# Attention's product of the last 64 keys on all 128 rows, and a planner that counts changes of array shape

## The chip, the cores and the metric

The kernel runs on one core of one Trainium2 chip. The metric is device time in microseconds of one execution. Times shown are of the whole program: attention and two feed-forward layers in one launch.

## The reference, cut to what matters

```python
# q, k, v: (4, 8, 576, 64), tau: 0.02
scores = scale * np.matmul(q, k.transpose(0, 1, 3, 2))
thresh = np.max(scores, axis=-1, keepdims=True) - tau
scores = np.where(scores >= thresh, scores, -1000000000.0)
attn = softmax(scores)                      # exp, divided by the row's sum
x = np.matmul(attn, v)                      # to (2304, 512)
h = x @ w_in;  x = (h * sigmoid(1.702 * h)) @ w_out      # 512 -> 2048 -> 512
h = x @ w_in2; x = (h * tanh(softplus(h))) @ w_out2      # 512 -> 2048 -> 512
```

All of it is float32. The change lies in attention; the two layers come after it and stay as they are.

## The kernel before, in words

**Tiling of attention.** Two heads are taken together (16 pairs of heads, `b` and `hp`). A pair has five groups of queries: four "full" ones of 128 queries of each head, and a "mixed" one that holds the last 64 queries of both heads, 64 rows each. That makes 80 groups. A group goes through four steps on TensorE and the engines behind it:

- `qk` (line 606): scores = q times k. Contraction over 64 rows, one head on rows 0 to 63 and the other on rows 64 to 127, so two small matmuls run side by side. Output in the PSUM tiles `sc`.
- `softmax_a` (line 635 on): VectorE scales, finds the maximum and cuts (L647, L657), GpSimd adds tau (L651), ScalarE takes the exponential (L654). The result is `p`, 576 keys beside each other, head 0 and then head 1.
- `turn` (line 679): TensorE transposes `p` in chunks of 128 keys into the PSUM banks `tb[0]`, `tb[1]`, `tb[2]` (L702). The keys 512 to 575, 64 of each head, are the "rest": one more transpose (L697), of 128 columns for a full group (both heads' rests together), of `m = 64` columns for a mixed one, which has one array of scores only. ScalarE copies the banks to SBUF (L717), the chunks to `pm`, the rest to `pmt`.
- `product` (line 722): transposed `p` times V (L752). For each of five chunks (`c`), two matmuls, one a head, write rows 0 to 63 and 64 to 127 of `av`. Chunks 0 to 3 contract over 128 rows. The rest (c = 4) contracts over 64: for a full product over rows `64 * i` to `64 * i + 63`, for a mixed one over rows 0 to 63. So the rest uses the array as 64 rows by 64 columns, the other chunks as 128 rows by 64 columns. Every float32 matmul leaves two records in the trace. A full product takes two groups at once (256 queries of one head), after every second full group. `av` lies in the halves of `tb[3]` for full products, and in columns 256 to 319 of `tb[2]` for mixed ones. ScalarE copies `av` out (L761).

So TensorE works in shapes, which the trace shows as rows*columns of a form: `64*128` and `64*64` (scores), `128*128` (transposes, and both layers), `128*64` (products, and the mixed rest's transpose), `64*64` (the rests' products).

**The order of the work.** Nothing is ordered by the hardware: `Order` (lines 53 to 196) is a planner. `add` (line 77) records each step with an engine, an estimated duration, what it reads and writes, and a rank. `run` (line 98) simulates the engines: each time an engine is free it takes, of the steps that are ready, the one of the lowest rank (the oldest one at equal rank). The times so found fix the order in which instructions are issued; a step of several matmuls (`steps`) is spread over its duration, and what other engines do in that time is issued in between. On the chip each engine then works through its own list in that order and waits where data are not ready. Ranks: scores of group g have g - 8 (`SF`), its transposes and copies g, a product g + 1.5 (`VR`), where g is the second of its two groups. The early part of `run` also fills TensorE with spare transposes until the first step of `turn` (`keep_warm`).

**Other work beside attention.** From group 40 on, the weights of the first layer are converted on ScalarE, VectorE and GpSimd (`load_w1`, lines L383 to L405), one f-block every five groups. V arrives by one DMA a pair of heads (`prep`, line 599); the host lays it out as 512 columns of the four chunks and 2 x 64 columns of rests (`tail`, line 980 on). After attention, layer 1 (L521, L566) and layer 2 (L521, L927) run on TensorE.

Of the kernel before, what the change touches and what calls it, by code (L numbers as in the profile page):

```python
# [11 lines left out]
F32 = mybir.dt.float32  # L12
# [9 lines left out]
DMA_RATE = 200e3  # L22
SF = 8
PR = 2
AR = 0.1
VR = 1.5
NORM_P = 1.0
# [15 lines left out]
NKQ = 2  # L43
# [9 lines left out]
class Order:  # L53
# [16 lines left out]
    def __init__(self):  # L70
        self.ops = []
        self.writer = {}
        self.readers = {}
        self.fill = None
        self.port = set()

    def add(self, eng, dur, fn, r=(), w=(), rank=0.0, deps=(), nbytes=None, port=False, steps=1):
        n = len(self.ops)
        if port:
            self.port.add(n)  # L80
        before = set(deps)
        for key in r:
            if key in self.writer:
                before.add(self.writer[key])
        for key in w:
            if key in self.writer:
                before.add(self.writer[key])
            before.update(self.readers.get(key, ()))
        for key in r:
            self.readers.setdefault(key, []).append(n)  # L90
        for key in w:
            self.writer[key] = n
            self.readers[key] = []
        before.discard(n)
        self.ops.append((eng, dur, fn, before, rank, nbytes, steps))
        return n

    def run(self):
# [10 lines left out]
        now = {e: [] for e in engines}  # L109
# [5 lines left out]
        wire = 0.0  # L115
        order = []
        port, done = 0.0, 0
        while done < n_ops:
            best = None
            for e in engines:  # L120
                if now[e]:
                    t = free[e]
                elif future[e]:
                    t = max(free[e], future[e][0][0])
                else:
                    continue
                if best is None or t < best[0]:
                    best = (t, e)
            t, e = best
            while future[e] and future[e][0][0] <= t:  # L130
                i = heapq.heappop(future[e])[1]
                heapq.heappush(now[e], (self.ops[i][4], i))
            aside = []
            i = None
            while now[e]:
                item = heapq.heappop(now[e])
                if item[1] in self.port and port > t + 1e-6:
                    aside.append(item)
                    continue
                i = item[1]  # L140
                break
            for item in aside:
                heapq.heappush(now[e], item)
            if i is None:
                free[e] = port
                continue
            done += 1
            _, dur, _, _, _, nbytes, _ = self.ops[i]
            free[e] = end = t + dur
            if i in self.port:  # L150
                port = end
            self.last = max(self.last, end)
            if nbytes is not None:
                wire = end = max(wire, end + DMA_US) + nbytes / DMA_RATE
            order.append((t, i))
            for a in after[i]:
                lat = self.LAT[e][self.ops[a][0]] if dur or nbytes else 0.0
                ready[a] = max(ready[a], end + lat + SLACK)
                left[a] -= 1
                if not left[a]:  # L160
                    heapq.heappush(future[self.ops[a][0]], (ready[a], a))
        self.order = order = sorted(order)
        if self.fill is not None:
            eng, until, dur, fn = self.fill
            at, gaps = 1.2, []
            for t, i in order:
                if i == until:
                    break
                if self.ops[i][0] == eng:
                    n = int((t - at - FG) / dur) if gaps else FI  # L170
                    if n > 0:
                        gaps.append((at, i, n))
                    at = t + self.ops[i][1]
            order = sorted([(t, i, 0) for t, i in order] + gaps)
        else:
            order = [(t, i, 0) for t, i in order]
        events = []
        for t, i, n in order:
            _, dur, fn, *_, steps = self.ops[i]
            if n:  # L180
                events.append((t, len(events), self.fill[3], n))
            elif steps == 1:
                events.append((t, len(events), fn))
            else:
                for k in range(steps):
                    events.append((t + dur * (k + 1) / steps, len(events), next_of, i, k))
# [16 lines left out]
def attention_then_two_ffn_kernel(  # L203
# [21 lines left out]
    nc = tc.nc  # L225
# [357 lines left out]


    kqs = Ring(apool, "kq", NKQ, [128, 2 * S], F32)
    vrs = Ring(apool, "vr", NKQ, [128, 5 * 128], F32)
    pps = Ring(apool, "p", NP // 2, [128, P1 + S + 1], F32)
    sss = Ring(apool, "ss", NSS, [128, S + 5], F32)
    nms = Ring(apool, "nm", 8, [128, 2], F32)
# [9 lines left out]
    def prep(b, hp, rank):  # L599
        kq2, kkq = kqs.next()  # L600
        vr, kvr = vrs.next()
        dma(lambda: nc.sync.dma_start(out=kq2, in_=kq[b, hp]), 589824, w=[kkq], rank=rank)
        dma(lambda: nc.sync.dma_start(out=vr, in_=v[b, hp]), 327680, w=[kvr], rank=rank)
        head[b, hp] = (kq2, vr, kkq, kvr)

    def qk(tl, rank):
# [5 lines left out]
        def mm():  # L612
# [13 lines left out]
                yield  # L626

        n = 4 if kind == "full" else 2
        add("PE", n * 0.25 + 0.25, mm, [kkq], [("sc", i) for i in range(n)], rank,
            steps=4 if kind == "full" else 5)  # L630
        return [(sc[i][:, :, 0:SH], [("sc", 2 * i), ("sc", 2 * i + 1)]) for i in range(n // 2)]

    def softmax_a(sums, ksum, col, rank, bank, pair, i):
# [45 lines left out]
    def turn(tl, ps, pair, rank):  # L679

        kind, b, hp, t = tl
        full = kind == "full"
        if t == 0:
            xo[b, hp] = xos.next()
        if full:
            if t % 2 == 0:
                turned[b, hp] = [pms.next(), pms.next(), pmt.next()]
            plan = [(0, (0, 1), 128), (1, (2, 3), 128), (2, (4,), 128)]
        else:
            turned[b, hp] = [pms.next(), pmt.next()]  # L690
            plan = [(0, (0, 1, 2, 3), 128), (1, (4,), 64)]

        def tr(bank, cs):
            for n, c in enumerate(cs):
                if c == 4:
                    m = 64 * len(ps)
                    nc.tensor.transpose(tb[bank][0:m, 0:128], pair[:, 516:516 + m], ident)  # L697
                    yield
                    continue
                for i in range(len(ps)):  # L700
                    a, c0 = (P1 + 64 if i else 4) + c * 128, (n * len(ps) + i) * 128
                    nc.tensor.transpose(tb[bank][:, c0:c0 + 128], pair[:, a:a + 128], ident)  # L702
                    yield

        for (bank, cs, rows), (pn, kpn) in zip(plan, turned[b, hp]):
            n = 1 if 4 in cs else len(ps) * len(cs)
            cols = 128 * n
            n = add("PE", n * 0.109 + (0.16 if bank == 0 else 0.0), lambda bank=bank, cs=cs: tr(bank, cs),
                ps, [("tb", bank)], rank, steps=max(n, 2))
            if sch.fill is None and WARM:  # L710
                sch.fill = ("PE", n, 0.107, keep_warm)
            src = tb[bank][0:rows, 0:cols]
            dst = pn[0:rows, 0:cols]
            if full:
                dst = pn[0:rows].rearrange("p (g q) -> p g q", q=256)[:, :, t % 2 * 128:t % 2 * 128 + 128]
                src = src.rearrange("p (g q) -> p g q", q=128)
            add("ACT", t_act(cols), lambda src=src, dst=dst: nc.scalar.copy(dst, src),  # L717
                [("tb", bank)], [kpn + (t % 2,)], rank)
        if not full or t % 2:
            product(tl, rank)  # L720

    def product(tl, rank):
# [17 lines left out]
        def mm(cs):  # L740
            for c in cs:
                for i in range(2):
                    rows, vc = slice(0, 128), c * 128 + 64 * i
                    if c < 4 and full:
                        p, a = pn[c // 2], (c % 2 * 2 + i) * 256
                    elif c < 4:
                        p, a = pn[0], c * 128 + i * 64
                    elif full:
                        rows, p, a, vc = slice(64 * i, 64 * i + 64), pn[2], 0, 512
                    else:  # L750
                        rows, p, a = slice(0, 64), pn[1], 64 * i
                    nc.tensor.matmul(  # L752
                        av[64 * i:64 * i + 64], vr[rows, vc:vc + 64], p[rows, a:a + w],
                        start=(c == 0), stop=(c == 4))
                    yield

        for cs, kp in parts:
            add("PE", len(cs) * (0.482 if full else 0.12) + 0.02, lambda cs=cs: mm(cs),
                kp + [kvr], [kav] + ["product"] * full, rank + VR, steps=2 * len(cs))
        x, kx = xo[b, hp]  # L760
        add("ACT", t_act(w), lambda: nc.scalar.copy(x[:, at:at + w], av), [kav],  # L761
            [kx + (j,) for j in ((t - 1, t) if full else (t,))], rank + VR)
# [252 lines left out]
```

## Time and profile before

| what | value |
|---|---|
| time, median of 3 runs | 1086.83 us (1086.48 to 1087.23) |
| the profiled execution, its own time | 1086.56 us |
| its span in the trace | 1084.8 us |
| TensorE matmul busy in the span | 1073.4 us (99%) |
| VectorE, ScalarE, GpSimd busy | 689.7, 647.8, 161.4 us |
| granted clock of TensorE | 1.0 throughout |
| matmuls of attention end, layer 1 begins | about 289 us; last attention matmul at 298.6 us |

"Busy" of TensorE counts each matmul from its start until its result is out, and matmuls overlap, so 99% doesn't say that the array is full. What a matmul costs a full queue is the distance from its start to the next one's start. In the timeline a row merges matmuls of one form: its first column is the first start, so the difference of the first columns of two neighbouring rows is what the earlier one cost the engine.

### The profile page before, as it was taken

The numbers are of one execution on the slowest core, as the hardware profiler recorded it, in microseconds if no ns is written. First come the engines' busy times: TensorE is split into PE (matmuls) and PEld (weight loads), VectorE is DVE, ScalarE is ACT, GpSimd is POOL, SyncE is SP. The second block draws the span as 40 slices with busy tenths as digits, with TensorE's granted clock in tenths as the row PEclk, the third lists the DMA queues.
The fourth block names the chain that finished last, engine by engine and source line by source line (L and its number), as shares of the span: only waits on it lengthen the run. The fifth ranks groups of instructions, "written<-read, shape, count | busy, mean of one in ns | idle before, by whom it ended". The sixth has DMA issues, their size and how long they took to land.

```text
span 1084.8 us, 16166 instructions
## 1 busy us (share of the span) xinstructions
PE 1073.4 (99%) x6068; PEld 844.8 (78%) x6068; DVE 689.7 (64%) x1378; ACT 647.8 (60%) x1033; POOL 161.4 (15%) x182
## 2 busy tenths in 40 slices
PE   9999999999999999999999999999999999999998
PEld 6666666666688888888888889888888888888887
DVE  7888989899978646545642236665555564555544
ACT  5776778888767344444432245686565656555665
POOL 2221223354425003211310000000000000000000
PEclk9999999999999999999999999999999999999999
DMA  2224243434164265374540025500010010010010
GB/s 90 70 68 125 90 129 123 131 115 130 40 198 141 82 220 178 139 257 143 181 142 20 1 80 178 190 1 22 8 40 0 11 39 1 1 40 1 1 39 20
DMA packets 51390, 94.44 MB, mean 87 GB/s; under 512 B 7280, under 2 KB 28016, under 8 KB 51312
## 3 DMA queue, kind: packets, MB, share of 16 engines
q1 hardware_dynamic: 51312, 93.42, 26.6%
q8 instruction: 47, 0.77, 0.3%
q14 instruction: 31, 0.25, 0.1%
HBM read 70.78 MB, written 22.62 MB: 86 GB/s over the span
## 4 chain that ended last, share of the span: by engine, by line
PE 98%; ACT 1%; DVE 0%; DMA 0%; issue 0%; SPq 0%; ACTq 0%; DVEq 0%
PE h L521 36%; PE tb L566 18%; PE tb L927 18%; PE tb L752 9%; PE sc L625 8%; PE tb L702 7%; PE tb L697 1%; DMA kq<-in_kq 0%; ACT pmt L717 0%; ACT p L654 0%; DVE p L657 0%; DVE ss L647 0%; ACT pm L717 0%; DVE o L939 0%; SPq L783 0%
## 5 line engine op out<-in xcount | busy, mean ns | idle before, releaser
L889 ACT ACTIVATE ms<-ms 128x512 f32<-128x512 f32 (+1 forms) x240 | 131.3, 583 | 129.4 <-DVE ms L874 128.3
L521 PE MATMUL h<-xa,wh 128*128 128x512 f32 (+1 forms) x640 | 181.7, 368 | 0.0
L521 PE MATMUL h<-x,wh 128*128 128x512 f32 (+1 forms) x640 | 181.0, 368 | 0.0
L521 PEld LDWEIGHTS h<-x,wh 128*128 128x128 f32 x640 | 116.5, 188 | 20.4
L521 PEld LDWEIGHTS h<-xa,wh 128*128 128x128 f32 x640 | 116.0, 189 | 20.3 <-issue 0.4
L547 ACT ACTIVATE t<-h 128x512 f32<-128x512 f32 (+1 forms) x80 | 44.4, 555 | 142.9 <-PE h L521 142.7
L657 DVE SCALAR_TENSOR_TENSOR p<-ss,nm,p 128x577 f32<-128x577 f32 x144 | 119.4, 851 | 14.5 <-ACT xo L761 6.1
L647 DVE TENSOR_SCALAR_CACHE_REDUCE ss<-sc,nqsc 128x576 f32<-128x576 f32 x144 | 112.4, 813 | 18.6 <-PE sc L625 17.9
L899 DVE TENSOR_TENSOR ms<-ms,hs 128x512 f32<-128x512 f32 (+1 forms) x80 | 50.1, 635 | 116.4 <-ACT ms L889 116.2
L550 DVE SCALAR_TENSOR_TENSOR h<-t,h 128x512 f32<-128x512 f32 (+1 forms) x80 | 51.2, 640 | 111.4 <-ACT t L547 111.2
L566 PE MATMUL tb<-gl,wh 128*128 128x512 f32 (+1 forms) x320 | 117.8, 368 | 0.0
L521 PE MATMUL h<-xa,wl 128*128 128x512 f32 (+1 forms) x320 | 117.7, 368 | 0.0
L566 PE MATMUL tb<-gh,wh 128*128 128x512 f32 (+1 forms) x320 | 117.7, 368 | 0.0
L521 PE MATMUL h<-x,wl 128*128 128x512 f32 (+1 forms) x320 | 117.7, 368 | 0.0
L566 PE MATMUL tb<-gh,wl 128*128 128x512 f32 (+1 forms) x320 | 117.7, 368 | 0.0
L654 ACT ACTIVATE p<-ss,nm 128x576 f32<-128x576 f32 x144 | 109.8, 785 | 11.2 <-DVE ss L647 11.1
L395 POOL TENSOR_TENSOR sv<-sv,sr 128x1024 uint32<-128x1024 uint32 x32 | 84.0, 2628 | 201.3 <-DVE sv L392 152.1
L927 PE MATMUL tb<-wh,g2h 128*128 128x512 f32 x288 | 112.1, 389 | 0.0
L927 PE MATMUL tb<-wl,g2h 128*128 128x512 f32 x288 | 112.1, 389 | 0.0
L927 PE MATMUL tb<-wh,g2l 128*128 128x512 f32 x288 | 112.0, 389 | 0.0
L651 POOL TENSOR_SCALAR nm<-nm,tau_p 128x1 f32<-128x1 f32 x144 | 76.8, 534 | 190.2 <-DVE ss L647 187.0
L889 ACT ACT_TABLE_LOAD x80 | 102.6, 1283 | 1.4
(59 smaller groups left out, 1685.6 us busy)
## 6 DMA issues: line engine op xcount, KB each, us to landing
sr<-in_w_in SPq DMA_DIRECT2D x32, 512.0 KB
sr<-in_w_out SPq DMA_DIRECT2D x32, 512.0 KB
kq<-in_kq SPq DMA_DIRECT2D x16, 576.0 KB
sv<-x_d SPq DMA_DIRECT2D x16, 512.0 KB
w_d<-sv SPq DMA_DIRECT2D x16, 512.0 KB
sv<-w_d SPq DMA_DIRECT2D x16, 512.0 KB
vr<-in_v SPq DMA_DIRECT2D x16, 320.0 KB
x_d<-xo SPq DMA_DIRECT2D x16, 288.0 KB
```

The lines of the kernel that those rows point to most:

```text
L395: lambda: nc.gpsimd.tensor_tensor(bits, bits, word(0), ALU.add), keys, [kval], rank, port=True)
L521: nc.tensor.matmul(hb[dst][:, 0:n], a[:, c, :], x[:, lo, c, 0:n], start=(i == 0), stop=(i == 3 * KD - 1))
L566: nc.tensor.matmul(accs[e][0][:, 0:n], a[:, es], b()[:, 0:n], start=(f == 0 and i == 0), stop=(f == KF - 1 and i == 2), skip_group_check=True,
L625: nc.tensor.matmul(dst, q, kq2[rows, k0:k0 + n], start=True, stop=True)
L647: lambda: nc.vector.tensor_scalar(n3, s3, nqsc, None, ALU.mult, ALU.min, accum_out=nm[:, 0:1]),
L651: lambda: nc.gpsimd.tensor_scalar(nm[:, 1:2], nm[:, 0:1], tau_p, 0.0, ALU.add, ALU.add),
L654: lambda: nc.scalar.activation(p[:, at:at + S], ns[:, 4:4 + S], AF.Exp, bias=nm[:, 0:1], scale=-1.0),
L657: lambda: nc.vector.scalar_tensor_tensor(p[:, whole], ns[:, 3 + i:4 + S + i], nm[:, 1:2], p[:, whole], ALU.is_le, ALU.mult, accum_out=sums ...
L702: nc.tensor.transpose(tb[bank][:, c0:c0 + 128], pair[:, a:a + 128], ident)
L752: nc.tensor.matmul(av[64 * i:64 * i + 64], vr[rows, vc:vc + 64], p[rows, a:a + w], start=(c == 0), stop=(c == 4))
L889: nc.scalar.activation(m()[:, 0:n], m()[:, 0:n], fn, bias=bias)
L927: nc.tensor.matmul(accs[t][0], x[:, t * 128:(t + 1) * 128], w, start=(f == 0 and i == 0), stop=(f == KF - 1 and i == 2), skip_group_check= ...
```

## The change

The rest's product takes all 128 rows, with zeros in V where a head has nothing; V gets a third tail column block for it. The mixed rest's transpose is 128 columns wide. In the planner, a step on TensorE carries a `mode` (0: transposes and the layers, 1: scores, 2: products). TensorE's choice among ready steps adds `KEEP` = 0.5 to the rank of a step of another mode than the last one, and such a step lasts `TURN` = 0.15 us longer. The estimates of the three kinds of step are new.

```diff
+KEEP = 0.5
+TURN = 0.15
...
+            if e == "PE":
+                item = min(now[e], key=lambda x: (x[0] + KEEP * (self.mode.get(x[1], 0) != held), x[1]))
+                now[e].remove(item)
+                heapq.heapify(now[e])
+                i = item[1]
+            while i is None and now[e]:
...
+            if e == "PE" and self.mode.get(i, 0) != held:
+                held = self.mode.get(i, 0)
+                dur += TURN
+            took[i] = dur
...
-    vrs = Ring(apool, "vr", NKQ, [128, 5 * 128], F32)
+    vrs = Ring(apool, "vr", NKQ, [128, 4 * 128 + 3 * D], F32)
...
-        dma(lambda: nc.sync.dma_start(out=vr, in_=v[b, hp]), 327680, w=[kvr], rank=rank)
+        dma(lambda: nc.sync.dma_start(out=vr, in_=v[b, hp]), 360448, w=[kvr], rank=rank)
...
-        add("PE", n * 0.25 + 0.25, mm, [kkq], [("sc", i) for i in range(n)], rank,
-            steps=4 if kind == "full" else 5)
+        add("PE", 1.02, mm, [kkq], [("sc", i) for i in range(n)], rank,
+            steps=4 if kind == "full" else 5, mode=1)
...
-                    m = 64 * len(ps)
-                    nc.tensor.transpose(tb[bank][0:m, 0:128], pair[:, 516:516 + m], ident)
+                    nc.tensor.transpose(tb[bank][:, 0:128], pair[:, 516:644], ident)
...
-            n = add("PE", n * 0.109 + (0.16 if bank == 0 else 0.0), lambda bank=bank, cs=cs: tr(bank, cs),
+            n = add("PE", n * 0.109, lambda bank=bank, cs=cs: tr(bank, cs),
...
-                    rows, vc = slice(0, 128), c * 128 + 64 * i
+                    vc = c * 128 + 64 * i
...
-                        rows, p, a, vc = slice(64 * i, 64 * i + 64), pn[2], 0, 512
+                        p, a = pn[2], 0
                     else:
-                        rows, p, a = slice(0, 64), pn[1], 64 * i
+                        p, a, vc = pn[1], 64 * i, 512 + 128 * i
                     nc.tensor.matmul(
-                        av[64 * i:64 * i + 64], vr[rows, vc:vc + 64], p[rows, a:a + w],
+                        av[64 * i:64 * i + 64], vr[:, vc:vc + 64], p[:, a:a + w],
...
-            add("PE", len(cs) * (0.482 if full else 0.12) + 0.02, lambda cs=cs: mm(cs),
-                kp + [kvr], [kav] + ["product"] * full, rank + VR, steps=2 * len(cs))
+            add("PE", len(cs) * (0.43 if full else 0.115), lambda cs=cs: mm(cs),
+                kp + [kvr], [kav] + ["product"] * full, rank + VR, steps=2 * len(cs), mode=2)
...
-    tail = _np.zeros((B, H // 2, 128, 2, D), v.dtype)
+    tail = _np.zeros((B, H // 2, 128, 3, D), v.dtype)
     for i in range(2):
-        tail[:, :, 64 * i:64 * i + 64, 0] = vh[:, :, i, 512:]
-    tail[:, :, :64, 1] = vh[:, :, 1, 512:]
+        tail[:, :, 64 * i:64 * i + 64, i] = vh[:, :, i, 512:]
+    tail[:, :, :64, 2] = vh[:, :, 1, 512:]
```

## Rows read from the trace of the kernel before

**Rows 1.** The profile page: the chain that ended last, share of the span by line.

```profile
PE h L521 36%; PE tb L566 18%; PE tb L927 18%; PE tb L752 9%; PE sc L625 8%; PE tb L702 7%; PE tb L697 1%; DMA kq<-in_kq 0%; ACT pmt L717 0%; ACT p L654 0%; DVE p L657 0%; DVE ss L647 0%; ACT pm L717 0%; DVE o L939 0%; SPq L783 0%
```

**Rows 2.** Windows: length; busy PE, PEld, DVE, ACT, POOL; clock, DMA share, GB/s.

```profile
25.00:150.00 125.00, 121.96 (x1006) 77.31 (x1007) 106.27 (x280) 91.62 (x187) 27.82 (x65) 1.00 0.31 91
150.00:288.00 138.00, 135.67 (x1118) 85.07 (x1117) 127.64 (x310) 116.81 (x223) 58.56 (x74) 1.00 0.37 118
```

**Rows 3.** Timeline of TensorE: start, us until the last end, line, form, count.

```profile
199.97 1.08 PE L752 MATMUL tb<-pm,vr 128*64 128x256 f32 x8
200.98 0.65 PE L752 MATMUL tb<-pmt,vr 64*64 64x256 f32 x4
201.56 1.09 PE L702 MATMUL tb<-ident,p 128*128 128x128 f32 x8
202.49 0.27 PE L697 MATMUL tb<-ident,p 128*128 128x128 f32 x1
202.69 1.24 PE L625 MATMUL sc<-kq 64*128 64x288 f32 x8
203.87 0.66 PE L702 MATMUL tb<-ident,p 128*128 128x128 f32 x4
204.36 0.27 PE L697 MATMUL tb<-ident,p 128*64 128x128 f32 x1
204.56 1.95 PE L752 MATMUL tb<-pm,vr 128*64 128x256 f32 x16
206.44 1.24 PE L625 MATMUL sc<-kq 64*128 64x288 f32 x8
207.61 0.65 PE L752 MATMUL tb<-pmt,vr 64*64 64x256 f32 x4
208.19 1.09 PE L702 MATMUL tb<-ident,p 128*128 128x128 f32 x8
...
210.60 0.69 PE L752 MATMUL tb<-pm,vr 128*64 128x64 f32 x16
211.71 0.33 PE L752 MATMUL tb<-pmt,vr 64*64 64x64 f32 x4 [0.42 <-ACT pmt L717]
```

**Rows 4.** The same timeline: first and last full rest right behind its chunks.

```profile
22.03 0.65 PE L752 MATMUL tb<-pmt,vr 64*64 64x256 f32 x4
...
287.15 0.65 PE L752 MATMUL tb<-pmt,vr 64*64 64x256 f32 x4
```

**Rows 5.** Line 752: records, ns of one (min/median/max), first and last start, forms.

```profile
L752 PEld LDWEIGHTS tb<-pm,vr x768: 132/137/138, 17.5 to 298.2; 128*64 128x64 f32 x192
```

**Rows 6.** Timeline of TensorE: a mixed product without a wait.

```profile
156.98 0.69 PE L752 MATMUL tb<-pm,vr 128*64 128x64 f32 x16
157.59 0.33 PE L752 MATMUL tb<-pmt,vr 64*64 64x64 f32 x4
157.86 0.66 PE L702 MATMUL tb<-ident,p 128*128 128x128 f32 x4
```

**Rows 7.** Waits: who waited for whom, us in total, times, longest.

```profile
PE tb L752 <- ACT pmt L717: 4.6, 11, 0.4
```

**Rows 8.** Timeline of TensorE: the first mixed rest whose wait lies at its own start.

```profile
52.01 0.33 PE L752 MATMUL tb<-pmt,vr 64*64 64x64 f32 x4 [0.42 <-ACT pmt L717]
```

**Rows 9.** Timeline of all engines: ScalarE's copy of a rest beside that product.

```profile
211.39 0.27 ACT L717 COPY pmt<-tb 128x128 f32<-128x128 f32 x1 [1.07 <-PE tb L752]
```

**Rows 10.** Timeline of TensorE: transposes that break a product, the first, one, the last.

```profile
18.57 0.66 PE L702 MATMUL tb<-ident,p 128*128 128x128 f32 x4
...
180.47 0.33 PE L697 MATMUL tb<-ident,p 128*128 128x128 f32 x1
180.73 1.08 PE L752 MATMUL tb<-pm,vr 128*64 128x256 f32 x8
...
293.60 0.66 PE L702 MATMUL tb<-ident,p 128*128 128x128 f32 x4
```

**Rows 11.** Groups by line and shape: count, busy us, mean ns; idle before.

```profile
L717 ACT COPY pm<-tb 128x512 f32<-128x512 f32 x144 | 79.7, 587 | 16.1 <-PE tb L702 15.2 <-ACT pm L717 0.2
```

More of the change, by code (lines that the diff above doesn't have):

```diff
@@ L75, in __init__, with add @@
         self.port = set()
-    def add(self, eng, dur, fn, r=(), w=(), rank=0.0, deps=(), nbytes=None, port=False, steps=1):
+        self.mode = {}
+    def add(self, eng, dur, fn, r=(), w=(), rank=0.0, deps=(), nbytes=None, port=False, steps=1, mode=0):
         n = len(self.ops)
+        if mode:
+            self.mode[n] = mode
         if port:
@@ L117, in run @@
         port, done = 0.0, 0
+        held, took = 0, {}
         while done < n_ops:
@@ L134, in run @@
             i = None
-            while now[e]:
+            if e == "PE":
[4 more added lines that the diff above has]
+            while i is None and now[e]:
                 item = heapq.heappop(now[e])
@@ L172, in run @@
                         gaps.append((at, i, n))
-                    at = t + self.ops[i][1]
+                    at = t + took[i]
             order = sorted([(t, i, 0) for t, i in order] + gaps)
@@ L178, in run @@
         for t, i, n in order:
-            _, dur, fn, *_, steps = self.ops[i]
+            _, _, fn, *_, steps = self.ops[i]
+            dur = took[i]
             if n:
@@ L687, in turn @@
                 turned[b, hp] = [pms.next(), pms.next(), pmt.next()]
-            plan = [(0, (0, 1), 128), (1, (2, 3), 128), (2, (4,), 128)]
+            plan = [(0, (0, 1)), (1, (2, 3)), (2, (4,))]
         else:
             turned[b, hp] = [pms.next(), pmt.next()]
-            plan = [(0, (0, 1, 2, 3), 128), (1, (4,), 64)]
+            plan = [(0, (0, 1, 2, 3)), (1, (4,))]
         def tr(bank, cs):
@@ L703, in tr @@
                     yield
-        for (bank, cs, rows), (pn, kpn) in zip(plan, turned[b, hp]):
+        for (bank, cs), (pn, kpn) in zip(plan, turned[b, hp]):
             n = 1 if 4 in cs else len(ps) * len(cs)
             cols = 128 * n
-            n = add("PE", n * 0.109 + (0.16 if bank == 0 else 0.0), lambda bank=bank, cs=cs: tr(bank, cs),
+            n = add("PE", n * 0.109, lambda bank=bank, cs=cs: tr(bank, cs),
                 ps, [("tb", bank)], rank, steps=max(n, 2))
@@ L711, in turn @@
                 sch.fill = ("PE", n, 0.107, keep_warm)
-            src = tb[bank][0:rows, 0:cols]
-            dst = pn[0:rows, 0:cols]
+            src = tb[bank][:, 0:cols]
+            dst = pn[:, 0:cols]
             if full:
-                dst = pn[0:rows].rearrange("p (g q) -> p g q", q=256)[:, :, t % 2 * 128:t % 2 * 128 + 128]
+                dst = pn.rearrange("p (g q) -> p g q", q=256)[:, :, t % 2 * 128:t % 2 * 128 + 128]
                 src = src.rearrange("p (g q) -> p g q", q=128)
@@ L979 @@
     vh = v.reshape(B, H // 2, 2, S, D)
-    tail = _np.zeros((B, H // 2, 128, 2, D), v.dtype)
+    tail = _np.zeros((B, H // 2, 128, 3, D), v.dtype)
     for i in range(2):
-        tail[:, :, 64 * i:64 * i + 64, 0] = vh[:, :, i, 512:]
-    tail[:, :, :64, 1] = vh[:, :, 1, 512:]
+        tail[:, :, 64 * i:64 * i + 64, i] = vh[:, :, i, 512:]
+    tail[:, :, :64, 2] = vh[:, :, 1, 512:]
     vl = _np.concatenate([
         vh[:, :, :, :512].reshape(B, H // 2, 2, 4, 128, D).transpose(0, 1, 4, 3, 2, 5).reshape(B, H // 2, 128, 512),
-        tail.reshape(B, H // 2, 128, 2 * D),
+        tail.reshape(B, H // 2, 128, 3 * D),
     ], axis=3)
```

## The prediction

> **What bounds the kernel now.** I start with the page's chain, the work that ended last followed back: it runs through TensorE's matmuls almost alone. The lines of attention (L625, L697, L702, L752) hold 25% of the span, the two layers 72% [rows 1]. Overlapping matmuls make such shares too kind, so I look next at windows of attention. From 25 to 150 us TensorE is idle for 3.0 us, from 150 to 288 us for 2.3. VectorE comes next: it rests for 18.7 us in the first stretch and for 10.4 in the second [rows 2]. So TensorE bounds attention as it bounds the layers. A microsecond saved on it in attention moves everything behind it forward, and the next limit is 10 us away in the tighter stretch.
>
> Then the timeline of TensorE, reading distances between starts. Eight product records cost 1.01 us when another shape follows (199.97 to 200.98), sixteen cost 1.88 (204.56 to 206.44). The eight more cost 0.87, so one chunk (two heads, two records each) is 0.435, and a stay in this shape has 1.01 - 0.87 = 0.14 on top. The rest right after it, in its own shape of 64 rows, costs 0.58 (200.98 to 201.56) [rows 3]. It has as many columns as a chunk, and costs 0.145 more. That is the price of one change of shape. From 199.97 to 208.19 the engine changes what it does eight times [rows 3]: one change a microsecond, a seventh of the time.
>
> **The change part by part.**
>
> *Full products' rest on 128 rows.* There are 32. In 18 the rest comes right behind other chunks of its product, as at 200.98 [rows 3]; the first of the 18 is at 22.03, the last at 287.15 [rows 4]. There a change of shape disappears: the rest becomes one more chunk, 0.435 instead of 0.58. 18 x 0.145 = **2.6 us**. The other 14 stand alone, as at 207.61. They change shape before and behind whatever their rows are, and a lone stay of one chunk costs 0.435 + 0.14 = 0.58, which is what it costs today [rows 3]: nothing. Nor do zero rows lengthen a matmul: with 64 rows and with 128 a lone rest and a chunk plus its change come out alike.
>
> The loads of weights could speak against it. Sixteen product records bring sixteen loads of 0.137 us [rows 5], 2.2 us of loads in a stay of 1.88 that also holds all passes [rows 3]. So the loads lie beside the passes although all use the same 128 rows. The Trainium skill (TensorE: Matmul & The Clock Gate, Part 3, "The mechanism") says that a load overlaps running matmuls only when its row group differs; the two halves of today's rest have different row groups, the new ones share theirs. By that rule the 192 loads of the 48 rests come into the open, an estimate of 192 x 0.137 = 26 us; by the row it is nothing. The trace contradicts the rule for this shape, so the sum goes without it.
>
> *Mixed products' rest.* There are 16. Without a wait, sixteen records cost 0.61 and the rest 0.27 [rows 6]. A chunk there is at most 0.61 / 4 = 0.15, so the rest saves at least 0.12, and at most the 0.145 of a change. But eleven of the sixteen are stalled: TensorE waits for ScalarE's copy to pmt [rows 7], and sixteen records take 1.11 instead of 0.61 (210.60 to 211.71) [rows 3]. In five of the eleven, the first at 52.01 [rows 8] and the last at 211.71 [rows 3], the wait lies exactly where the shape changes and hides the change: nothing saved. In the other six it lies inside the first sixteen records. 11 x 0.12 = **1.3 us**.
>
> *Mixed rest's transpose 128 wide.* A 64-wide transpose at 204.36 starts 0.49 after the first of the four 128-wide ones ahead of it. A 128-wide one starts 0.93 after the first of eight (202.49 after 201.56). The four more account for 0.44, 0.11 each, so going to 64 columns costs no change of shape. What follows starts 0.20 later in both cases (204.56, 202.69) [rows 3]. So **0**. ScalarE's copy gets 128 rows instead of 64. A copy of 128 rows takes 0.27 [rows 9]; if half of it were new, sixteen would take 2.2 us more of ScalarE, which is idle for over 20 us in each stretch [rows 2]. Uncovered it would be that 2.2.
>
> *V.* Each of the 16 loads grows from 327,680 to 360,448 bytes, with as many issues on SP as before. At the 91 GB/s of the first stretch the 32 KB more take 0.36 us, and the DMA engines are in use for a third [rows 2]. V is double-buffered a pair of heads ahead: 0, and 16 x 0.36 = 5.8 if each lay open.
>
> *The planner.* Its new figures (0.15 a change, 0.43 a chunk) are what I read above. Where can KEEP alter a choice? Scores rank g - 8 and go first whenever ready; half a rank doesn't matter there. Between a product (g + 1.5) and the next group's transposes (g + 1), the product now ties if TensorE holds that mode, and wins as the older step. Today six products are broken by transposes, from 18.57 to 293.60. At 180.47 one transpose takes 0.26 between two halves [rows 10], though its own share is 0.11. Joined, each saves two changes, 0.29; six give 1.7 at most. I can't see which of them the new order joins, and take half, **0.9 us**.
>
> The new estimates shift all later times of the plan, so the stalls are dealt anew. One costs 1.11 - 0.61 = 0.50 [rows 3, 6], eleven 5.5. All could vanish; I bound a loss by as many new ones. Between -5.5 and +5.5 I take 0, as no row leans either way.
>
> *Sum.* 2.6 + 1.3 + 0.9 = 4.8 us off the profiled 1086.56 (a span of 1084.8 and 1.8 around it): **1081.8 us**. The median of the runs stands 0.3 above the profiled one. A measurement of this kernel can tell about 0.2%, 2.2 us, from no change.
>
> **The rivals.**
>
> *The stalls vanish too.* A full group's rest and the mixed product lie in different columns of the same bank, tb[2]. At 211.39 ScalarE's copy of the rest starts after 1.07 us of waiting for the mixed product [rows 9], and then the last part of that product waits for the copy. It comes from the order of issue: the copy was issued amid the product's matmuls. For it: five of sixteen have no stall. Against it: the product lasts longer in the plan (0.575 + 0.15 instead of 0.62), so a copy falls into it as easily. If all go, 1081.8 - 5.5 = 1076.3. Chance 0.16.
>
> *Nothing comes of it.* The new order may part rests from their products more often than in 14 of 32 (then the 0.145 isn't earned: the change doesn't do what it says), or the time saved turns into waits for VectorE, which has 10.4 us left in the second stretch [rows 2]. With no saving 1086.6, with a third of it 1085.0. Chance 0.17.
>
> *Slower: transposes come too late.* If a held product goes ahead of the mixed group's transposes, these come directly before their own product, which then waits for copies of 0.587 [rows 11] and 0.27 [rows 9], 0.86 a pair of heads. Today a full product's sixteen records lie between, at 204.56, and their 1.88 covers the copies [rows 3]. For it: the tie. Against it: where scores come just before, the transposes still win by half a rank. With ten of sixteen pairs uncovered, 8.6 lost and 3.9 saved: 1091.3. From eight pairs on (6.9 lost, 3.0 net) it is slower by more than the 2.2. Chance 0.11.
>
> *Loads in the open.* If a load had to wait until its rows were free, 192 x 0.137 = 26 us less the 3.9 would give 1109. The sixteen loads within 1.88 us speak against it [rows 3, 5]. Chance 0.02. The skill's sentence on row groups, above, is this rival.
>
> *The narrow transpose is a change of shape after all.* Then each of the sixteen could save 0.145 more, 2.3 in all: 1079.5. The 0.49 and the 0.20 worked out above speak against it [rows 3]. Chance 0.03. The Trainium skill (TensorEngine Tiling (Array Packing), Tiling Modes, "Key Properties") says that changing the tiling mode drains TensorE. For products and rests the trace agrees (0.145 a change); for this transpose it shows no such cost.
>
> **How the numbers follow.** The forecast has 0.51; its own range is 1079.5 to 1084.4 (all or none of the broken products, and about a third more or less on the rests). Faster by over 0.2%: 0.51 + 0.16 + 0.03 = 0.70. Within 0.2%: 0.17. Slower: 0.11 + 0.02 = 0.13. The range takes in the forecast, the vanishing stalls and no effect, 1076.0 to 1087.0, and leaves out the 0.13 and some edges.
>
> **What would show it.** Right: no 64*64 form on L752, and 960 records of 128*64 instead of 768; twenty records in one stay, with 1.88 + 0.435 = 2.3 to the next block; a mixed product without a stall 0.73 to 0.76 to the next block (0.88 today); layer 1 begins near 284 us, and what follows lasts as long as before. Wrong: four product records alone in more than 14 places; the wait for the pmt copy in other than 11 places; new waits of TensorE for pm copies or VectorE; neighbouring chunks' records more than 0.22 apart where nothing is waited for.

## The result, and the profile after

The changed kernel takes 1076.85 us (median of 4 runs, 1076.28 to 1077.33) where the kernel before takes 1087.03. The ratio is 0.9906 (95% interval 0.9889 to 0.9923): 10.2 us less, 0.8 to 1.1%. The forecast was 1081.8 with a range from 1076.0 to 1087.0. The direction is right and the time lies just inside the range; the gain is twice the forecast one.

The page of the changed kernel, its span, its engines and the chain by line (lines have moved: L752 is now L767, L625 is L641, L697 and L702 are L712 and L717, L717 is L732):

```profile
span 1074.5 us, 16198 instructions
PE 1063.5 (99%) x6068; PEld 847.3 (79%) x6068; DVE 686.2 (64%) x1378; ACT 646.0 (60%) x1033; POOL 166.6 (16%) x182
PE h L537 36%; PE tb L582 18%; PE tb L942 18%; PE sc L641 8%; PE tb L767 7%; PE tb L717 6%; PE tb L712 1%; ACT pm L732 1%; ACT p L670 1%; DVE p L673 1%; DVE ss L663 1%; DMA kq<-in_kq 0%; DVE wl L421 0%; ACT sv L399 0%; ACT sr L401 0%
```

Each engine runs as many instructions as before. The chain is no longer matmuls alone: ScalarE's copies (pm) and exponentials and VectorE's two softmax steps hold 1% each, where [rows 1] showed 0%. The conversions (sv, wl) appear in it, at 0%; in [rows 1] they are not listed.

Where the time went is told by the end of attention. The first layer matmul after the last product, in the kernel before and then in the changed one:

```profile
298.70 0.50 PE L521 MATMUL h<-xa,wh 128*128 128x512 f32 x1
```

```profile
288.30 0.74 PE L537 MATMUL h<-xa,wh 128*128 128x512 f32 x2
```

From there to the end of the span are 786.1 us (1084.8 - 298.7) and 786.2 (1074.5 - 288.3). Layer 1 begins ahead of that, at 288.69 and at 274.77, but in both kernels 24 of its matmuls stand ahead of the last product, so the two distances compare like with like. Attention is 10.4 us shorter and the layers take as long as before.

One pair of heads in the changed kernel, from one mixed product to the next. To be set beside [rows 3]:

```profile
28.34 0.65 PE L767 MATMUL tb<-pmt,vr 128*64 128x256 f32 x4
28.82 0.63 PE L767 MATMUL tb<-pm,vr 128*64 128x64 f32 x16
29.29 0.29 PE L767 MATMUL tb<-pmt,vr 128*64 128x64 f32 x4
29.50 1.09 PE L717 MATMUL tb<-ident,p 128*128 128x128 f32 x8
...
34.06 1.95 PE L767 MATMUL tb<-pm,vr 128*64 128x256 f32 x16
...
38.24 0.65 PE L767 MATMUL tb<-pmt,vr 128*64 128x256 f32 x4
38.83 1.09 PE L717 MATMUL tb<-ident,p 128*128 128x128 f32 x8
...
41.02 0.33 PE L712 MATMUL tb<-ident,p 128*128 128x128 f32 x1
41.19 0.60 PE L717 MATMUL tb<-ident,p 128*128 128x128 f32 x4
...
41.83 1.95 PE L767 MATMUL tb<-pm,vr 128*64 128x256 f32 x16
43.70 1.24 PE L641 MATMUL sc<-kq 64*128 64x288 f32 x8
44.87 0.65 PE L767 MATMUL tb<-pmt,vr 128*64 128x256 f32 x4
45.36 0.63 PE L767 MATMUL tb<-pm,vr 128*64 128x64 f32 x16
45.82 0.29 PE L767 MATMUL tb<-pmt,vr 128*64 128x64 f32 x4
```

And the starts of two such mixed products in the kernel before:

```profile
33.14 0.45 PE L752 MATMUL tb<-pm,vr 128*64 128x64 f32 x8
...
50.91 0.69 PE L752 MATMUL tb<-pm,vr 128*64 128x64 f32 x16
```

Two things are new. The mixed product (45.36) comes right behind the rest of a full product (44.87), in the same shape; in [rows 3] it stood at 210.60 behind a lone transpose. That is so in 12 of the 16 pairs. And there is no wait: from 28.82 to 45.36 a pair takes 16.54 us, where it took 17.77 (33.14 to 50.91). Counted record by record in the traces of all of attention, scores, transposes and products give way to each other 222 times instead of 270 (the plan counts 226 for the changed kernel), and no rest has a shape of its own any more (before, 34 rests changed shape inside a product: 18 full, 16 mixed).

TensorE's waits and its idle time by stretch in the changed kernel, beside [rows 7] and [rows 2]:

```profile
PE tb L717 <- ACT pm L732: 2.8, 6, 1.2
PE tb L767 <- ACT pmt L732: 0.8, 2, 0.4
```

```profile
25.00:150.00 125.00, 125.00 (x1091) 83.39 (x1089) 111.85 (x293) 96.42 (x201) 32.95 (x69) 1.00 0.32 102
150.00:285.00 135.00, 129.90 (x1068) 86.17 (x1067) 129.56 (x306) 115.00 (x217) 61.70 (x72) 1.00 0.38 121
```

Nine of the eleven stalls at the pmt copy are gone, and from 25 to 150 us TensorE is never idle. Behind that it is idle for 5.1 us, more than before, and waits six times for the pm copies, where the kernel before did so once, for 0.5 us. So the gain of the first half does not go on through the second, where the weight conversions run.

### The profile page after: what moved, and what is told of

It reads as the page before. It is cut to its first block, busy times and chain, and to the rows that moved or that the text cites. A ratio compares the mean times of both kernels' runs of the same rounds, so it can differ in the third digit from the quotient of the medians.

```text
span 1074.5 us, 16198 instructions
## 1 busy us (share of the span) xinstructions
PE 1063.5 (99%) x6068; PEld 847.3 (79%) x6068; DVE 686.2 (64%) x1378; ACT 646.0 (60%) x1033; POOL 166.6 (16%) x182
## 4 chain that ended last, share of the span: by engine, by line
PE 94%; ACT 2%; DVE 2%; issue 1%; DMA 0%; SPq 0%; ACTq 0%; DVEq 0%
PE h L537 36%; PE tb L582 18%; PE tb L942 18%; PE sc L641 8%; PE tb L767 7%; PE tb L717 6%; PE tb L712 1%; ACT pm L732 1%; ACT p L670 1%; DVE p L673 1%; DVE ss L663 1%; DMA kq<-in_kq 0%; DVE wl L421 0%; ACT sv L399 0%; ACT sr L401 0%
## 5 line engine op out<-in xcount | busy, mean ns | idle before, releaser
L667 POOL TENSOR_SCALAR nm<-nm,tau_p 128x1 f32<-128x1 f32 x144 | 81.5, 567 | 170.8 <-DVE ss L663 165.9
```

What stands on the lines that cost most here:

```text
L667: lambda: nc.gpsimd.tensor_scalar(nm[:, 1:2], nm[:, 0:1], tau_p, 0.0, ALU.add, ALU.add),
```

## The experiments

My theory after the result: the rests gave what the forecast said, and the order gave the remaining 6 us, by fewer changes and fewer stalls, with a part of it lost again to waits after 150 us. The rival: the rests gave it all, or the new estimates did.

**The array part alone.** The rests, the wide transposes and V's layout of the change, with the planner as it was; the issue order is that of the kernel before.

```diff
-                        rows, p, a, vc = slice(64 * i, 64 * i + 64), pn[2], 0, 512
+                        p, a = pn[2], 0
...
-                        rows, p, a = slice(0, 64), pn[1], 64 * i
+                        p, a, vc = pn[1], 64 * i, 512 + 128 * i
```

> The rests on 128 rows and the 128-wide transposes, with the planner of before, which issues everything in the order of before. If the working for the rests holds (18 full rests at 0.145 us, 11 mixed at 0.12), 3.9 us below the kernel before, about 1083.1, and the eleven waits for the pmt copy stay. If a change of shape is worth nothing once something else is waited for, 1087. If the array part were the whole of it, 1077.

Measured: 1083.09 us (0.9964, 0.995 to 0.9978: the ratio to the kernel before in the same session, and its 95% interval), 3.7 below the 1086.76 of the kernel before there. Its wait for the pmt copy is what it was:

```profile
PE tb L751 <- ACT pmt L716: 4.6, 11, 0.4
```

The working for the rests stands. The 6.2 us from here to the changed kernel (1076.85) are the planner's, and the two intervals lie apart.

**The planner alone.** The changed kernel's planner and issue order, rests and transposes in the shapes of before.

```diff
-                        p, a = pn[2], 0
+                        rows, p, a, vc = slice(64 * i, 64 * i + 64), pn[2], 0, 512
...
-                        p, a, vc = pn[1], 64 * i, 512 + 128 * i
+                        rows, p, a = slice(0, 64), pn[1], 64 * i
```

> The new planner, whose order is that of the changed kernel, with the rests in their old shape of 64 rows. If the gain beyond the forecast comes from the order, most of it stays. Sixteen places (a full rest followed by a mixed product and its rest) get two more changes of shape, 32 x 0.145 = 4.6 us over the changed kernel: about 1081.5. If the order gains nothing by itself, 1087.

Measured: 1080.87 (0.9944, 0.9929 to 0.9959). The order gains 5.9 alone. The 32 changes of shape cost 4.0 us against the changed kernel, 0.126 each; the intervals of the two kernels lie apart. The trace of one pair, to compare with 44.87 to 45.82 above:

```profile
45.61 0.65 PE L769 MATMUL tb<-pmt,vr 64*64 64x256 f32 x4
46.19 0.69 PE L769 MATMUL tb<-pm,vr 128*64 128x64 f32 x16
46.80 0.33 PE L769 MATMUL tb<-pmt,vr 64*64 64x64 f32 x4
47.06 0.66 PE L718 MATMUL tb<-ident,p 128*128 128x128 f32 x4
```

A full rest and the mixed product behind it take 1.45 here (45.61 to 47.06), and 1.16 in the changed kernel (28.34, where the rest of four begins, to 29.50).

**Preference or estimates?** The changed kernel without the preference, and the changed kernel with it but with the estimates of before.

```diff
-KEEP = 0.5
+KEEP = 0.0
```

> The changed kernel without the preference for the mode held (KEEP = 0); the new estimates and the 0.15 us a change stay in the plan. The plan has 258 changes of shape instead of 226. If changes and stalls are the price: 32 x 0.145 = 4.6 us, plus two to four stalls of 0.5 (transpose, then mixed product): 1081.5 to 1083.5. If the new estimates carry the gain and the preference none, 1077.

```diff
-TURN = 0.15
+TURN = 0.0
...
-        add("PE", 1.02, mm, [kkq], [("sc", i) for i in range(n)], rank,
+        add("PE", n * 0.25 + 0.25, mm, [kkq], [("sc", i) for i in range(n)], rank,
...
-            n = add("PE", n * 0.109, lambda bank=bank, cs=cs: tr(bank, cs),
+            n = add("PE", n * 0.109 + (0.16 if bank == 0 else 0.0), lambda bank=bank, cs=cs: tr(bank, cs),
...
-            add("PE", len(cs) * (0.43 if full else 0.115), lambda cs=cs: mm(cs),
+            add("PE", len(cs) * (0.482 if full else 0.12) + 0.02, lambda cs=cs: mm(cs),
```

> The changed kernel with the preference kept, but the estimates of before and no 0.15 us in the plan (TURN = 0). The plan has 234 changes of shape, eight more than the changed kernel: 8 x 0.145 = 1.2 us, about 1078. If exact estimates are what makes the order good (by sparing waits), clearly more, 1080 or above.

This last kernel is the one that later expectations call the fourth of the first set.

Measured: 1083.93 without the preference (0.9975, 0.9965 to 0.9984), 1074.11 with it and the old estimates (0.9883, 0.9868 to 0.9897). So the preference carries the order's gain: on top of the array part it is worth 9.0 us, while the new estimates (with the 0.15 a change) lose 0.8 without it and 2.7 with it. The 0.8 is less than these intervals can tell. Of the 2.7 they leave little doubt: they overlap by a hair, but the four runs with the old estimates (1073.86 to 1074.36) lie wholly below the four of the changed kernel (1076.28 to 1077.33). So the best kernel here has the preference and the old estimates. Their waits of TensorE for the pmt copy, without the preference and with it (there the row is missing, and this one is the largest in attention):

```profile
PE tb L767 <- ACT pmt L732: 5.0, 12, 0.4
```

```profile
PE sc L641 <- DVE ss L663: 2.0, 4, 0.9
```

Without the preference the mixed product falls back behind transposes in 14 of the 16 pairs, and twelve stalls are there. Where the 2.7 us lie, the second stretch of the kernel with the old estimates suggests:

```profile
150.00:285.00 135.00, 132.59 (x1093) 87.46 (x1089) 131.15 (x303) 113.75 (x216) 59.77 (x73) 1.00 0.35 114
```

TensorE is idle for 2.4 us there, and for 5.1 in the changed kernel.

**What a stall is worth by itself.** The array part alone, with a mixed product's ten matmuls issued in one go, so that no copy can be issued amid them.

```diff
-            add("PE", len(cs) * (0.482 if full else 0.12) + 0.02, lambda cs=cs: mm(cs),
-                kp + [kvr], [kav] + ["product"] * full, rank + VR, steps=2 * len(cs))
+            add("PE", len(cs) * (0.482 if full else 0.12) + 0.02,
+                (lambda cs=cs: mm(cs)) if full else (lambda cs=cs: list(mm(cs))),
+                kp + [kvr], [kav] + ["product"] * full, rank + VR, steps=2 * len(cs) if full else 1)
```

> The array part alone (order and planner of before), but the ten matmuls of a mixed product are issued in one go, so that ScalarE's copy of a full rest is issued before or after them, not amid them. If the eleven stalls come from the interleaved issue: 11 x 0.50 = 5.5 us, and five rests whose cost a wait had hidden give 0.6 more: 1083.1 - 6.1 = 1077.0, with no wait for the pmt copy on the product. If the product or its successor waits for the same copy elsewhere, 1083.

Measured: 1082.54 (0.9958, 0.9943 to 0.9973; the runs spread from 1081.07 to 1083.56). The stalls at the product are gone, but of the 6.1 us only 0.6 are gained in the median, 2.0 in the fastest run, which is the one profiled: a miss. The trace shows where much of it went:

```profile
102.16 0.69 PE L751 MATMUL tb<-pm,vr 128*64 128x64 f32 x16
102.68 0.29 PE L751 MATMUL tb<-pmt,vr 128*64 128x64 f32 x4
102.90 1.09 PE L701 MATMUL tb<-ident,p 128*128 128x128 f32 x8
104.16 0.33 PE L696 MATMUL tb<-ident,p 128*128 128x128 f32 x1 [0.18 <-ACT xo L761]
```

The next full rest's transpose starts 1.26 after the first of its eight, not 0.93 [rows 3]: it writes tb[2] and waits until ScalarE has copied the mixed product out of the same bank. It happens seven times, some 0.33 each, 2.3 us. So the interleaved issue does put the stall into the product, but without it the shared bank makes a smaller wait at its next user. In the changed kernel a whole product and 4.3 us lie between a full group's rest going into tb[2] (41.02) and the mixed product that uses the same bank (45.36).

**Narrow transposes.** The changed kernel with the mixed rest's transposes 64 wide.

```diff
-                    nc.tensor.transpose(tb[bank][:, 0:128], pair[:, 516:644], ident)
+                    m = 64 * len(ps)
+                    nc.tensor.transpose(tb[bank][0:m, 0:128], pair[:, 516:516 + m], ident)
```

> The changed kernel with the mixed rest's transpose 64 columns wide again. If a narrow transpose costs no change of shape, the same as the changed kernel, 1076.9, within 0.5. If it does, up to 16 x 2 x 0.145 = 4.6 us more, 1081.5.

Measured: 1076.14 (0.99, 0.9886 to 0.9915). The narrow ones cost nothing; if anything they are 0.7 us better, which these intervals can't separate.

**The waits after 150 us.** One such wait in the changed kernel, first TensorE and then ScalarE:

```profile
189.69 0.27 PE L712 MATMUL tb<-ident,p 128*128 128x128 f32 x1
191.21 0.55 PE L717 MATMUL tb<-ident,p 128*128 128x128 f32 x3 [1.24 <-ACT pm L732]
```

```profile
188.49 1.19 ACT L399 ACTIVATE sv<-sr 128x1024 f32<-128x1024 f32 x1
189.55 1.14 ACT L401 ACTIVATE sr<-sr 128x1024 f32<-128x1024 uint32 x1
190.57 1.07 ACT L732 COPY pm<-tb 128x512 f32<-128x512 f32 x2
```

Two conversion steps of over 1 us stand on ScalarE ahead of the copies that free the transposes' banks. Is it the load, or the order? First the same load spread over all of attention, then less load in the same order.

```diff
-C0 = 40
-C1 = 5
+C0 = 5
+C1 = 10
```

> The changed kernel with the eight weight conversions spread over all of attention (from group 5 on, every ten groups, instead of from group 40 on, every five). If the gain stops after 160 us because the conversions fill VectorE and ScalarE there, the waits of the second half shrink: some 4 us below the changed kernel, about 1073. If the waits come from the plan's order and not from the load, 1077 or no clear difference.

```diff
+        def cut(a):
+            return a[:, 0:8] if layer == 1 and f < 8 else a
...
-            lambda: nc.gpsimd.tensor_tensor(bits, bits, word(0), ALU.add), keys, [kval], rank, port=True)
+            lambda: nc.gpsimd.tensor_tensor(cut(bits), cut(bits), cut(word(0)), ALU.add), keys, [kval], rank, port=True)
```

(and likewise L401 on ScalarE and the three steps on VectorE)

> The changed kernel with the plan and order untouched, but five of the eight instructions of each of the first eight weight conversions work on 8 columns only (one on ScalarE, three on VectorE, one on GpSimd), so these weights are wrong. VectorE loses 8 x 2.8 us of work and ScalarE 8 x 1.2. If the waits that the changed kernel has after 160 us come from the conversions' load, they shrink and the time is 3 to 5 us lower, 1072 to 1074. If the plan's order alone makes them, 1077 within 0.7.

Measured: 1076.94 for the spread load (0.9907, 0.9892 to 0.9921), 1073.37 for the lighter one (0.9875, 0.986 to 0.9889). The windows of the two kernels, spread and lighter:

```profile
25.00:150.00 125.00, 123.23 (x1064) 81.65 (x1064) 117.36 (x291) 102.37 (x204) 43.72 (x68) 1.00 0.38 123
150.00:285.00 135.00, 133.00 (x1090) 88.07 (x1091) 125.09 (x312) 109.03 (x213) 54.60 (x74) 1.00 0.36 113
```

```profile
150.00:285.00 135.00, 132.39 (x1098) 88.10 (x1096) 113.18 (x313) 111.44 (x223) 37.72 (x73) 1.00 0.41 129
```

With the same order and less load TensorE is idle for 2.6 us instead of 5.1 and the time falls by 3.5: in this order the load makes half of the waits. Spreading the load moves more of them than it removes (1.8 idle before 150 us, where there was none, 2.0 behind), and what is removed doesn't show in the time; the order that results has three more changes in the trace, 225. The load isn't the whole of it, though: the kernel with the old estimates carries the full load in another order and is idle for 2.4 us in that stretch, above.

**Other estimates and preferences.** Three variants asked whether truer estimates or a stronger preference give more.

```diff
-        add("DVE", t_dve(S) + 0.075,
+        add("DVE", t_dve(S) + 0.23,
...
-        add("DVE", t_dve(S) + 0.08,
+        add("DVE", t_dve(S) + 0.26,
...
-        return (0.05 if psum else 0.09) + n * 0.833e-3 + 0.093 * ptr
+        return (0.16 if psum else 0.21) + n * 0.833e-3 + 0.093 * ptr
```

> The changed kernel with the plan's durations of VectorE's and ScalarE's steps in attention raised to what the trace shows (0.11 to 0.18 us each). The plan has 241 changes of shape, 15 more than the changed kernel: +2.2 us. If the waits that the changed kernel has gained come from these short estimates, they go (some 4 us): about 1075. If they don't, 1079.

The last line (`t_act`) also serves ScalarE's conversions and the layers, whose estimates grew with it. The next has TensorE's estimates of before and no 0.15 a change, the same two VectorE lines, and 0.11 to 0.12 more on ScalarE's steps of attention alone.

> The preference with TensorE's estimates of before (as in the fourth kernel of the first set, 1074.1), and VectorE's and ScalarE's steps of attention alone at the durations of the trace (0.11 to 0.18 us more each); conversions and layers keep their estimates. The plan has 234 changes of shape, as many as there. If short estimates are behind the waits after 160 us, some 2 us less, 1072; if not, 1074 or a little more.

```diff
-KEEP = 0.5
+KEEP = 2.0
```

> As the fourth kernel of the first set (preference, estimates of before), with KEEP = 2 instead of 0.5. The plan has 228 changes of shape instead of 234. If changes are all that matters, 6 x 0.145 = 0.9 us less, 1073.2. If a longer stay in one shape makes transposes late, waits eat it: 1074 to 1077.

Measured: 1096.81 (1.0087, 1.0071 to 1.0104), 1095.26 (1.0074, 1.0059 to 1.0089) and 1076.09 (0.9899, 0.9883 to 0.9916). KEEP = 2 is 2.0 slower than KEEP = 0.5 although it changes shape less often; TensorE's waits are 1.8 us longer, 0.8 of that for the pmt copy. The first two are slower than the kernel before, and my premise was wrong. I had read VectorE's durations as its cost. In the changed kernel's trace:

```profile
187.23 0.80 DVE L673 SCALAR_TENSOR_TENSOR p<-ss,nm,p 128x577 f32<-128x577 f32 x1
187.97 0.81 DVE L673 SCALAR_TENSOR_TENSOR p<-ss,nm,p 128x577 f32<-128x577 f32 x1
```

A step lasts 0.80, but the next one starts after 0.74, and 0.74 is what the plan had. With 0.16 to 0.18 us too much for each of 288 steps the conversions come later: their last step on VectorE (L421) runs three times and twice before 285 us in these two kernels, and six times in the changed one. That the plan believes VectorE full is my reading. Both runs raised ScalarE's steps as well, and no run raised one engine's alone, so the loss of some 20 us is of both together. The two largest waits of TensorE in the second kernel are then in layer 1:

```profile
PE h L537 <- ACT x L522: 6.2, 1, 6.2
PE h L537 <- DVE wl L421: 3.8, 7, 0.6
```

**Counting changes in the plan's time.** The last run takes TURN alone out of the changed kernel.

```diff
-TURN = 0.15
+TURN = 0.0
```

> The changed kernel with the preference and the new estimates, but no 0.15 us for a change in the plan (TURN = 0). The plan has 235 changes of shape instead of 226: 9 x 0.145 = 1.3 us, 1078.1, if counting them in the plan's time does nothing but lower their number. If the plan then believes TensorE faster than it is and packs conversions in otherwise, the waits of the second half decide, between 1074 (as the old estimates gave) and 1081.

Measured: 1090.07 (1.0029, 1.0018 to 1.0041), slower than the kernel before and outside what either expectation gave. Its windows in layer 1:

```profile
285.00:330.00 45.00, 45.00 (x226) 37.02 (x223) 35.09 (x42) 29.57 (x39) 15.62 (x6) 1.00 0.52 177
330.00:380.00 50.00, 42.56 (x179) 32.45 (x177) 37.91 (x41) 25.42 (x33) 16.54 (x5) 1.00 0.41 131
380.00:387.00 7.00, 5.03 (x11) 3.65 (x12) 2.61 (x4) 1.92 (x3) 0.00 (x0) 0.52 0.42 114
387.00:400.00 13.00, 13.00 (x58) 10.73 (x58) 7.09 (x12) 6.78 (x10) 2.43 (x1) 1.00 0.57 194
```

TensorE is idle for 7.4 us from 330 to 380, waiting for weights and x, and for 2.0 in the next seven, where its clock is low as well. Attention isn't longer: its last product ends about where it did (the next layer matmul starts at 287.28, 288.30 in the changed kernel). The conversions come later. Their last step on VectorE from 150 to 285 us, in the changed kernel and then in this one:

```profile
L421 DVE TENSOR_TENSOR wl<-sv,wh 128x1024 fp32r<-128x1024 f32 x6 | 9.5, 1584 | 0.0
L421 DVE TENSOR_TENSOR wl<-sv,wh 128x1024 fp32r<-128x1024 f32 x3 | 3.7, 1220 | 0.0
```

So the 0.15 in the plan's time does more than lower the number of changes, it moves the conversions forward. My explanation, which no run shows by itself: with estimates that leave out the changes the plan is shorter than the chip's time and has less room for conversions in attention. The old estimates have no such term either, but longer steps, and five of these conversion steps come before 285 us with them. What in them makes the order that waits 2.7 us less after 150 us stays open, and the old estimates together with the 0.15 were not run.

## Why the prediction was right, and where its size was off

*Bound by TensorE in attention, the layers unchanged:* right, 786.1 and 786.2 us.

*The rests, 2.6 + 1.3 = 3.9 us:* right, 3.7 by the array part alone. All 960 records of the products have the form 128*64 (768 and 192 by line and tile), and twenty records in one stay cost 2.31 (175.05 to 177.36), as forecast:

```profile
175.05 1.95 PE L767 MATMUL tb<-pm,vr 128*64 128x256 f32 x16
176.83 0.60 PE L767 MATMUL tb<-pmt,vr 128*64 128x256 f32 x4
177.36 0.33 PE L717 MATMUL tb<-ident,p 128*128 128x128 f32 x1
```

A mixed product behind a lone transpose and without a stall takes 0.74 to the next block (102.16 to 102.90, above), within the 0.73 to 0.76 of the forecast.

*Loads in the open* and *the narrow transpose as a change of shape:* both fell. The working on the loads had a flaw: it added up durations that overlap one another. In the mixed product of the changed kernel sixteen loads, 2.2 us by that sum, lie within 0.71:

```profile
45.14 0.71 PEld L767 LDWEIGHTS tb<-pm,vr 128*64 128x64 f32 x16
```

So neither the 2.2 nor the 26 us was a length of time; that the rests' loads cost nothing is shown by the array part's 3.7 us. A rest on 128 rows that stands alone takes 0.59 (38.24 to 38.83), as the 64-row one did at 207.61 [rows 3], and one behind its chunks 0.53 with the change that follows (176.83 to 177.36 in the trace), where 0.58 stood before.

*The planner, 0.9 us:* this is the term that was far too small. On "Today six products are broken by transposes" it counted only places where a product is cut, and valued the tie there. The same tie ("the product now ties if TensorE holds that mode, and wins as the older step") acts once a pair of heads at another place: a mixed product ties with the next pair's transposes and goes right behind the full rest. That joins two stays in 12 of the 16 pairs, and takes the mixed product away from the lone transpose, whose copy it collided with. Measured, the order is worth 6.2 us on top of the rests. Between the trace of the array part alone and that of the changed kernel lie 46 changes (268 and 222), which at 0.126 to 0.145 would be 5.8 to 6.7 of it. The vanished stalls then about pay for the new waits, and the windows say the same: TensorE's idle time is 3.0 + 2.3 us before [rows 2] and 0 + 5.1 after. This split is worked out from rows; no run has the fewer changes without the fewer stalls.

*Stalls, between -5.5 and +5.5, taken as 0, and the rival "the stalls vanish too" (1076.3):* the rival came nearest in time (1076.3 against 1076.85), but partly by luck. Nine of eleven stalls went, which is one of the signs of being wrong that the prediction named (the wait in other than 11 places); new waits for pm copies are another. The prediction named the shared bank and put the stall down to the order of issue. That is half of it: the run with the product in one go lost the stalls, and the bank gave 2.3 of their 5.5 us back as waits elsewhere. In the changed kernel they went because another product lies between. And the gain was given back: TensorE is idle for 5.1 us in the second stretch against 2.3 before. The time came out near the rival's because the changes of shape, which it did not count, brought about as much.

*VectorE as the next limit, "10 us away":* in the second stretch VectorE is busy for 129.56 of 135 now, so 5.4 us are still free. Yet TensorE waits already, most of all for ScalarE's pm copies (2.8 us). With lighter conversions 3.5 us more come off.

*Slower, by late transposes:* no sign of it up to 150 us; between a mixed group's transposes (41.19) and its product (45.36) lies the full product at 41.83, as before.

Layer 1 begins at 274.8 us, not near 284, because a part of it now runs ahead of the last products. The ends of the forecast's own range come out at 1079.7 and 1084.0 from the terms named, not 1079.5 and 1084.4; nothing hangs on it.

## What to carry to other kernels

Where one engine works in several shapes, count its changes over a whole period of the schedule, and ask at each tie who now goes first: here the order was worth more (6.2 us) than the shape of the rests (3.7). A planner's estimates do two things: they choose the order, and they decide how early work for the next stage is fitted in. So a variant is judged by the next stage's waits too. VectorE's steps had the distance between starts in the plan; with durations in its place, for VectorE and ScalarE together, the kernel was 20 us slower. Estimates read from a trace are not better in every case: those for TensorE, with the 0.15 a change, came out 2.7 us behind the old ones. A stall from a shared bank went when other work came between its two users; issuing their instructions apart moved part of it to the bank's next user.

## What was not expected of the hardware

VectorE's durations in the trace overlap: 0.80 us of duration and 0.74 from start to start for a step of 577 elements. The Trainium skill (Perfetto Trace Analysis, "Optimizing Scalar/DVE Operations") says that an instruction's fixed overhead of data access keeps VectorE busy for about 60 ns on SBUF and shows in the profiled latency at about twice that, since the acknowledging of the write overlaps with the next instruction; the trace agrees, with a difference of 0.06 us.

In the last run TensorE stood idle for 6.2 us, waiting for x, until 381.5 us. From 380 to 387 us the granted clock is 0.52 in the mean, close to the lower of the two levels (1.2 of 2.4 GHz), and from 387 to 400 it is 1.00 again. The kernel before and the changed one stay at 1.00 in these stretches.
